# GLU output projection as seven products of 256 columns per index pair, placed behind a pass's quads, in a fused attention, rational and GLU kernel

## The chip, the cores and the metric

The kernel runs on one core of a Trainium2 chip. The metric is the device time of one execution in microseconds (us), median of the runs shown; lower is better. TensorE (PE, its weight loads shown as PEld), VectorE (DVE), ScalarE (ACT), GpSimd (POOL) and SyncE (SP, which issues all DMAs here) each run their own instructions in order and wait for each other by semaphores. SBUF is the on-chip memory, PSUM the banks into which TensorE writes.

## The reference, cut to what matters

```python
# attention with pooled keys and values, then x: 4608 tokens x 512
h = x @ w_in; P = a0 + a1*h + a2*h**2 + a3*h**3          # w_in: 512 x 2048
Q = 1 + abs(b0)*abs(h) + abs(b1)*h**2
x = (P / (Q + 1e-6)) @ w_out                              # the rational part
gate = 1 / (1 + np.exp(-(x @ w_gate)))                    # 512 x 1536
val  = x @ w_val                                          # 512 x 1536
out  = (gate * val) @ w_out2                              # 1536 x 512: the last projection
```

All of it is float32.

## The kernel before

**The rational part** covers attention and the first pair of projections. It runs 144 steps (`NB` = 9 blocks of 512 tokens by `NF1` = 16 slices of 128 hidden columns). A step is 12 matmuls of `g1` (hidden slice, bank h), a chain of ACT and DVE instructions to `y`, the split of `y` into a high part (ACT) and a low part `g` (POOL, L630), and 12 matmuls of `g2` (banks acc). Every product of float32 data is made as three TensorE passes, high by high, high by low and low by high. The order of this part is not written out: each instruction is handed to a planner (`Planner`) with an engine, a cost, a rank and its buffers, and the planner lays out the five engines' orders by these numbers. In the background of it, `background(u, ...)` for u = 0 to 11 reads a slice of the GLU's weights, converts it (`conv1`: two ACT, one DVE and one POOL instruction of 512 columns), makes the sums of weight blocks for seven products (`POOL`, L388), splits them (ACT L396, POOL L398) and stores them to DRAM (`w2d`). It also converts and splits slice u of `w_out2` (`conv2` with POOL, L309) and stores it (`wo2d`). The u-th is ranked at step 32 + 8u.

**The GLU part** is written out by hand. It has `NP` = 6 passes of 768 tokens, a pass in two halves of `HB` = 384 tokens. For each of `NS` = 6 index pairs `s_` (256 hidden columns as 2 slices of 128) a `gate` quad and a `value` quad are made. A quad forms a 2 by 2 block result, two hidden slices by two token halves, out of seven products (`ORDER`) with sums of weights and of inputs; it has 42 matmuls of 384 columns (6 per product). Its weights come through a ring of `NQ` = 6 tiles of 512 KB, 42 loads a pass. DVE adds the products up from PSUM (`quad_sums`, L897), ACT makes the sigmoid, and `value` multiplies and splits the result at once: two multiplications on DVE and two on POOL (L957), the high parts on ACT (L857), the low parts on POOL (L860). The split results are the stationary operand of the last projection: `h2(f, h, a)` does 3 token tiles by 3 matmuls of 512 columns for hidden slice f and token half h. The split `w_out2` lies in SBUF throughout (12 tiles). Half 0 is projected between the quads (`h2A(s_ - 1, p)`, behind `gate(s_, p)`), half 1 behind the last quad of the pass; between the two stands `x_prep`, which makes the seven input operands of the next pass (four sums on DVE, seven high parts on ACT, seven low parts on POOL, each of 768 columns). `h2_out` copies the finished 512-column banks out and stores them.

The quads take their banks from four "h" banks and at times b7; accA holds b4 to b6. A pass has 504 matmuls of 384 columns and 216 of 512.

## Time and profile before

| what | value |
|---|---|
| median of 3 runs (1762.6 to 1764.45) | 1762.63 us |
| profiled execution, its own time | 1762.16 us |
| its span, first to last instruction | 1760.4 us |
| granted TensorE clock, mean | 0.996 |
| matmuls in it | 9072 |

The span is 1.76 us short of the execution's own time. A page of the profile gives the busy time of each engine and the granted clock in 40 slices; a row of a timeline is a start, a duration, an engine, a line and what is written and read; a row of a window gives the busy time of each engine in a stretch. The duration of a matmul or a weight load in the trace is longer than its pace, since such instructions overlap: the pace is the distance between starts.

### The profile page before, as it was taken

What the parts mean: (1) busy time and instruction counts of PE and PEld (TensorE: products, weight loads), DVE (VectorE), ACT (ScalarE), POOL (GpSimd) and SP (SyncE); (2) the same over time, 40 slices, a digit from 0 to 9 for tenths busy, and PEclk for the clock granted to TensorE, in tenths of its full rate; (3) what the DMA queues carried; (4) which work ended last, traced back from release to release, by engine and by line L of the source; (5) the groups of instructions that cost most, each with busy time, mean ns of one, the idle gap of its engine ahead of it and who ended that gap; (6) DMA issues with size and microseconds to landing.
All of it is one profiled execution on the core that took longest, in us unless ns stands there. A gap on an engine that the chain in (4) does not pass through costs nothing.

```text
span 1760.4 us, 25436 instructions
## 1 busy us (share of the span) xinstructions
PE 1737.6 (99%) x9072; PEld 1524.8 (87%) x9072; DVE 1074.3 (61%) x1731; ACT 967.7 (55%) x1746; POOL 800.3 (45%) x827
## 2 busy tenths in 40 slices
PE   7899999999999999999999999999999999999999
PEld 6688888888888888888889999999998998998997
DVE  6998888888888878887874433443343333433341
ACT  5999778787888887877763222223223222222221
POOL 6675256464655745545522433344234324424331
PEclk8999999999999999999999999999999999999999
DMA  7685454556535554543755754764663763763660
GB/s 239 192 273 200 144 195 159 198 173 208 191 135 203 178 190 157 180 144 138 233 174 166 237 160 156 235 184 143 221 204 124 240 184 125 242 193 112 206 197 36
DMA packets 133329, 319.89 MB, mean 182 GB/s; under 512 B 20948, under 2 KB 51668, under 8 KB 133204
## 3 DMA queue, kind: packets, MB, share of 16 engines
q1 hardware_dynamic: 133204, 318.28, 55.6%
q8 instruction: 72, 1.18, 0.3%
q14 instruction: 53, 0.43, 0.1%
HBM read 263.20 MB, written 54.00 MB: 180 GB/s over the span
## 4 chain that ended last, share of the span: by engine, by line
PE 92%; ACT 3%; DVE 2%; DMA 2%; issue 0%; POOL 0%; SPq 0%; ACTq 0%; DVEq 0%
PE h L591 17%; PE h L593 17%; PE h L592 17%; PE acc L591 7%; PE acc L593 7%; PE acc L592 7%; PE accA L976 3%; PE accA L977 3%; PE h L977 3%; PE h L976 3%; PE accA L975 3%; PE h L975 3%; PE sc L540 2%; PE psx L576 2%; PE pta L565 1%
## 5 line engine op out<-in xcount | busy, mean ns | idle before, releaser
L897 DVE TENSOR_TENSOR t<-h,t 128x384 f32<-128x384 f32 x360 | 200.7, 557 | 376.7 <-ACT t L911 243.5
L630 POOL TENSOR_TENSOR g<-y,g 128x512 fp32r<-128x512 f32 x144 | 188.1, 1306 | 255.8 <-ACT g L629 196.8
L957 POOL TENSOR_TENSOR t<-t 128x384 f32<-128x384 f32 x72 | 84.2, 1170 | 439.7 <-issue 245.4
L591 PE MATMUL h<-xs,wi 128*128 128x512 f32 x576 | 229.6, 399 | 3.2 <-DVE wi L309 1.9
L591 PE MATMUL acc<-g,wo 128*128 128x512 f32 x576 | 230.6, 400 | 0.0
L593 PE MATMUL acc<-g,wo 128*128 128x512 f32 x576 | 224.9, 390 | 0.6 <-POOL g L630 0.6
L593 PE MATMUL h<-xs,wi 128*128 128x512 f32 x576 | 225.4, 391 | 0.0
L592 PE MATMUL h<-xs,wi 128*128 128x512 f32 x576 | 225.3, 391 | 0.0
L592 PE MATMUL acc<-g,wo 128*128 128x512 f32 x576 | 224.6, 390 | 0.0
L591 PE MATMUL h<-xS,wq 128*128 128x384 f32 x576 | 192.9, 335 | 0.6 <-DVE y L627 0.6
L593 PE MATMUL h<-xS,wq 128*128 128x384 f32 x576 | 192.9, 335 | 0.0
L592 PE MATMUL h<-xS,wq 128*128 128x384 f32 x576 | 192.7, 334 | 0.0
L911 ACT ACTIVATE t<-h 128x384 f32<-128x384 f32 x72 | 35.4, 492 | 243.2 <-PE h L593 240.6
L617 ACT ACTIVATE u<-h,coef 128x512 f32<-128x512 f32 x144 | 98.9, 687 | 88.5 <-PE h L593 87.9
L625 DVE SCALAR_TENSOR_TENSOR y<-y,coef,h 128x512 f32<-128x512 f32 x144 | 107.0, 743 | 62.1 <-ACT h L624 61.7
L591 PE MATMUL h<-xA,wq 128*128 128x384 f32 x432 | 144.4, 334 | 0.0
L593 PE MATMUL h<-xA,wq 128*128 128x384 f32 x432 | 144.3, 334 | 0.0
L592 PE MATMUL h<-xA,wq 128*128 128x384 f32 x432 | 144.3, 334 | 0.0
L619 DVE SCALAR_TENSOR_TENSOR u<-u,coef,h 128x512 f32<-128x512 f32 x144 | 106.8, 742 | 55.4 <-ACT y L618 54.2
L591 PEld LDWEIGHTS h<-xs,wi 128*128 128x128 f32 x576 | 108.9, 189 | 26.2 <-issue 2.6
L591 PEld LDWEIGHTS acc<-g,wo 128*128 128x128 f32 x576 | 108.2, 188 | 24.6 <-issue 3.4
L593 PEld LDWEIGHTS h<-xs,wi 128*128 128x128 f32 x576 | 108.8, 189 | 23.8
(119 smaller groups left out, 4090.9 us busy)
## 6 DMA issues: line engine op xcount, KB each, us to landing
wq<-w2d SPq DMA_DIRECT2D x252, 512.0 KB
wo<-wod SPq DMA_DIRECT2D x96, 512.0 KB
w2d<-stage SPq DMA_DIRECT2D x36, 512.0 KB
stage<-in_moe_w_out_dram SPq DMA_DIRECT2D x28, 512.0 KB
out_dram<-o SPq DMA_DIRECT2D x36, 256.0 KB
rawk<-in_k_dram SPq DMA_DIRECT2D x32, 256.0 KB
rawq<-in_q_dram SPq DMA_DIRECT2D x32, 256.0 KB
rawv<-in_v_dram SPq DMA_DIRECT2D x32, 256.0 KB
```

What stands on the lines that cost most here:

```text
L591: nc.tensor.matmul(out_, wl, xh, start=start, stop=False, skip_group_check=on)
L592: nc.tensor.matmul(out_, wh, xh, start=False, stop=False, skip_group_check=on)
L593: nc.tensor.matmul(out_, wh, xl, start=False, stop=stop, skip_group_check=on)
L617: ACT(0.57, rank, lambda: nc.scalar.activation(u.t, h.t, AF.Abs, scale=coef[:, 5:6]), w=[u], r=[h, coef_b])
L619: plan("DVE", 0.66, rank, lambda: STT(out=u.t, in0=u.t, scalar=coef[:, 4:5], in1=h.t, op0=ALU.add, op1=ALU.mult), w=[u], r=[h])
L625: plan("DVE", 0.66, rank, lambda: STT(out=y.t, in0=y.t, scalar=coef[:, 0:1], in1=h.t, op0=ALU.add, op1=ALU.mult), w=[y], r=[h])
L630: plan("POOL", 1.3, rank, lambda: nc.gpsimd.tensor_tensor(out=g.t[:, 1], in0=y.t, in1=g.t[:, 0].bitcast(F32), op=ALU.subtract), w=[(g, 1)] ...
L897: nc.vector.tensor_tensor(out=out_, in0=a, in1=b, op=ALU.add)
L957: eng.tensor_tensor(out=y, in0=x, in1=y, op=ALU.mult)
L975: nc.tensor.matmul(a[t], gh, wt[:, 0], start=(f == 0), stop=False)
L976: nc.tensor.matmul(a[t], gh, wt[:, 1], start=False, stop=False)
L977: nc.tensor.matmul(a[t], gl, wt[:, 0], start=False, stop=(f == NF2 - 1))
```

## The change

**The last projection** is made by the same seven-product scheme. The 2 by 2 blocks are two token halves by two hidden slices of a pair, times two hidden slices by two halves of 256 output columns; for each index pair that gives seven products of 3 token tiles by 3 matmuls of 256 columns. They run in `h2(p)` behind all twelve quads of a pass, kind by kind (`H2`): six index pairs of product 1, six of product 2, and so on, 42 units of 9 matmuls, 378 matmuls a pass. Two sets of three banks take turns (X and Y). At the end of a kind `cut` takes the banks out: ACT copies for kinds 1, 6 and 5, DVE additions and stores for kinds 2, 7 and 3, a copy and a store for kind 4, all of 256 columns.

**The operands** of it: `value` now writes the products of gate and value unsplit into twelve pairs of SBUF tiles (`ga`, `gx`), POOL adds one pair of blocks, and `first` makes the split of the operand of kind 1 (ACT high, POOL low) and a difference on POOL. The other 36 units are split in `h2` by `prep`, six units ahead: high part on ACT (L878), low part on DVE (L881); for kinds 5 and 7 DVE makes a difference first (L971), nine units ahead. Ahead of the unit loop `prep` is called for units 6 to 11, and the loop calls it for the same six again, so a pass has 42 such splits. Ahead of the loop the splits of units 9 to 11 wait for the matmuls of units 0 to 2, whose tiles they take.

**The weights** of it are no longer kept in SBUF. `item_load` reads 512 KB for two units at a time, six loads ahead, 21 a pass, on SP.

**x_prep** no longer has a place of its own: two sums go to POOL behind `value(3)` (`X_EARLY`), the other nine jobs stand between the units of `h2` (`X_AT`), with the low parts and the two sums on DVE.

**In the rational part** `background` no longer handles `w_out2`. `background_out(u, ...)`, ranked at step 100 + 3u, reads half of the rows' columns for a pair, converts it (`conv1`), makes four blocks of sums on POOL (L422: one instruction of 256 columns, two of 128), splits seven blocks of 128 columns (ACT and POOL, L427 and L429, in instructions of 512, 128 and 256) and stores seven pieces of 128 KB. The inputs of the first pass (`rawx`, the operands) are made eight steps later than before (`BX`).

```diff
+    def background_out(u, r0, gate_on):
...
+        conv1(raw, r0 + 2)
...
+            plan("POOL", pool(P * len(o)), r0 + 3, sub, w=[(t2, x) for x in o], r=rw + [(t2, x - 1) for x in o if x in (1, 3)])
...
+                plan("ACT", act(P * m), r0 + 3, lambda x=x, m=m, at=at, g=g: nc.scalar.activation(g.t[:, x:x + m, 0], at(), AF.Copy), w=[(g, (x, 0))], r=rt)
+                plan("POOL", pool(P * m), r0 + 3, lambda x=x, m=m, at=at, g=g: nc.gpsimd.tensor_tensor(
+                    out=g.t[:, x:x + m, 1], in0=at(), in1=g.t[:, x:x + m, 0].bitcast(F32), op=ALU.subtract), w=[(g, (x, 1))], r=rt + [(g, (x, 0))])
...
         def value(s_, p):
+            a12, a21, a11, a22 = (ga[m, s_] for m in ("12", "21", "11", "22"))
+
+            def first():
+                ops[s_] = o = op_tile(s_)
+                split_hi(o, a11)
+                split_lo(o, a11, nc.gpsimd)
+                sub(a11, a21, a11, nc.gpsimd)
...
+        H2 = ((1, "11", 0), (2, "12", 1), (6, "11", 0), (5, "21", 1), (7, "11", 0), (3, "12", 1), (4, "22", 0))
+        UNITS = [(k, m, s_) for k, m, _ in H2 for s_ in range(NS)]
...
+        def prep(x):
+            if x + 3 < len(UNITS):
+                k, m, s_ = UNITS[x + 3]
+                if k == 5:
+                    sub(ga["12", s_], ga["12", s_], ga["11", s_], nc.vector)
+                elif k == 7:
+                    sub(ga["11", s_], ga["22", s_], ga["11", s_], nc.vector)
+            if NS <= x < len(UNITS):
+                m, s_ = UNITS[x][1:]
+                ops[x] = o = op_tile(x)
+                split_hi(o, ga[m, s_])
+                split_lo(o, ga[m, s_], nc.vector)
+
+        def h2_mm(p, x, a, t):
...
+            nc.tensor.matmul(a, gh, wh, start=s_ == 0 and not on, stop=False, skip_group_check=on)
+            nc.tensor.matmul(a, gh, wl, start=False, stop=False, skip_group_check=on)
+            nc.tensor.matmul(a, gl, wh, start=False, stop=s_ == NS - 1, skip_group_check=on)
...
+            for x in range(NS, NS + AHEAD2):
+                prep(x)
...
+                for s_ in range(NS):
+                    x = g * NS + s_
+                    prep(x + AHEAD2)
+                    for t in range(HT):
+                        h2_mm(p, x, a, t)
+                    if x % 2:
+                        item_load(p * 7 * NS // 2 + x // 2 + NQ)
+                    if p + 1 < NP and x in X_AT:
+                        x_prep(X_LATE[X_AT.index(x)])
+                for t in range(HT):
+                    cut(t)
...
+        AHEAD2 = 6
...
             for s_ in range(1, NS):
                 gate(s_, p)
-                h2A(s_ - 1, p)
                 value(s_, p)
...
-            aB = [new_bank() for t in range(HT)]
-            for f in range(4):
-                h2(f, 1, aB)
-            if p + 1 < NP:
-                for x in range(4):
-                    x_prep(x)
-            h2A(NS - 1, p)
-            h2_out(p, 0, accA.pop(p))
-            for f in range(4, NF2):
-                h2(f, 1, aB)
-            h2_out(p, 1, aB)
+            h2(p)
```

How instructions stand now at three places. First TensorE at the end of a gate quad (xS is its last input operand, h its banks), before:

```order
L592 MATMUL h<-xS_8981,wq 128x384
L593 MATMUL h<-xS_8981,wq 128x384
L975 MATMUL accA<-wo_8978,gA 128x512
L976 MATMUL accA<-wo_8978,gA 128x512
L977 MATMUL accA<-wo_8978,gA 128x512
```

and with the change:

```order
L619 MATMUL h<-xS_9476,wq 128x384
L620 MATMUL h<-xS_9476,wq 128x384
L618 MATMUL h<-xS_9370,wq 128x384
L619 MATMUL h<-xS_9370,wq 128x384
L620 MATMUL h<-xS_9370,wq 128x384
```

The 18 matmuls of the projection that stood between the gate quad and the value quad are gone; the value quad follows at once.

Second VectorE from the last instructions of a pass's last value quad, in the first pass. Before (rawx are the input sums of `x_prep`, o the copies of `h2_out`, and then the next pass's quads):

```order
L957 TENSOR_TENSOR t<-t 128x384
L873 TENSOR_TENSOR rawx<-rawx 128x768 x4
L984 COPY o<-accA 128x512
L984 COPY o<-h 128x512
L897 TENSOR_TENSOR t<-h,t 128x384 x8
```

and with the change (go are the low parts for the projection, x the low parts of the next pass's inputs, L971 a difference):

```order
L989 TENSOR_TENSOR gx<-t 128x384
L881 TENSOR_TENSOR go<-ga,go 128x384 x2
L881 TENSOR_TENSOR go<-gx,go 128x384 x4
L881 TENSOR_TENSOR go<-ga,go 128x384 x2
L881 TENSOR_TENSOR go<-gx,go 128x384
L881 TENSOR_TENSOR xA_10533<-rawx,xA_10533 128x768
L881 TENSOR_TENSOR go<-gx,go 128x384 x3
L881 TENSOR_TENSOR go<-ga,go 128x384
L898 TENSOR_TENSOR rawx<-rawx 128x768
L881 TENSOR_TENSOR go<-ga,go 128x384 x2
L971 TENSOR_TENSOR ga<-ga 128x384
```

DVE had six instructions between the quads of two passes; now it starts on a row of splits, of which the seventh is the first that unit 6 needs, and goes on with the inputs of the next pass between them.

Third GpSimd in the rational part near step 114 of 144. Before (g is the low part of a step, e the attention, stage the weights):

```order
L630 TENSOR_TENSOR g<-y,g 128x512
L398 TENSOR_TENSOR stage<-stage 128x256
L309 TENSOR_TENSOR stage<-stage 128x512
L630 TENSOR_TENSOR g<-y,g 128x512
L557 TENSOR_TENSOR e<-e,r 128x8x72
```

and with the change:

```order
L657 TENSOR_TENSOR g<-y,g 128x512
L398 TENSOR_TENSOR stage<-stage 128x256
L422 TENSOR_TENSOR stage<-stage 128x2x128
L398 TENSOR_TENSOR stage<-stage 128x256
L422 TENSOR_TENSOR stage<-stage 128x128 x2
L429 TENSOR_TENSOR stage<-stage 128x4x128
L657 TENSOR_TENSOR g<-y,g 128x512
```

Between two low parts of steps stood two background instructions; now six stand there, the new sums (L422) and splits (L429) among them.

## Rows read from the trace of the kernel before

**Rows 1.** Page: span; TensorE's busy time; granted clock in 40 slices, in tenths.

```profile
span 1760.4 us, 25436 instructions
PE 1737.6 (99%) x9072; PEld 1524.8 (87%) x9072; DVE 1074.3 (61%) x1731; ACT 967.7 (55%) x1746; POOL 800.3 (45%) x827
PEclk8999999999999999999999999999999999999999
```

**Rows 2.** TensorE's waits from 900 us on: us in total, times, longest.

```profile
PE h L591 <- DVE y L627: 0.6, 1, 0.6
```

**Rows 3.** Windows: stretch, length, PE PEld DVE ACT POOL busy (instructions), clock, DMA share, GB/s.

```profile
943.39:1044.23 100.84, 100.84 (x553) 97.12 (x552) 39.49 (x66) 25.95 (x54) 32.94 (x32) 1.00 0.70 219
1044.23:1072.83 28.60, 28.60 (x127) 23.65 (x127) 9.57 (x8) 7.87 (x12) 18.15 (x12) 1.00 0.18 62
300.00:700.00 400.00, 399.85 (x2070) 329.55 (x2069) 332.05 (x549) 324.08 (x584) 227.73 (x272) 1.00 0.54 182
1520.00:1540.00 20.00, 20.00 (x111) 19.26 (x110) 8.03 (x14) 4.94 (x11) 7.57 (x8) 1.00 0.85 284
```

**Rows 4.** Timeline of TensorE: start us, duration us, line, tiles.

```profile
506.02 1.14 PE L540 MATMUL sc<-kbd,rawq 128*128 128x144 f32 x8
...
1018.22 0.33 PE L591 MATMUL h<-xS,wq 128*128 128x384 f32 x1
...
1032.81 0.39 PE L975 MATMUL accA<-wo,gA 128*128 128x512 f32 x1
...
1036.93 0.33 PE L591 MATMUL h<-xS,wq 128*128 128x384 f32 x1
...
1044.23 0.39 PE L975 MATMUL h<-wo,gB 128*128 128x512 f32 x1
...
1072.83 0.33 PE L591 MATMUL h<-xS,wq 128*128 128x384 f32 x1
```

**Rows 5.** One line's view, 500 to 508 us: duration min/median/max, first and last start.

```profile
L540 PE MATMUL sc<-kbd,rawq x8: 283/286/286, 506.0 to 506.9; 128*128 128x144 f32 x8
```

**Rows 6.** Groups of weight loads: line, tiles, shape, count, busy us, mean ns.

```profile
L540 PEld LDWEIGHTS sc<-kbd,rawq 128*128 128x128 f32 x320 | 46.1, 196 | 9.2 <-issue 3.2 <-ACT kbd L449 1.7 <-PE psx L576 1.3
L975 PEld LDWEIGHTS accA<-wo,gA 128*128 128x128 f32 x216 | 40.6, 188 | 7.8
```

**Rows 7.** Groups from 900 us on: line, tiles, shape, count, busy us, mean ns.

```profile
L897 DVE TENSOR_TENSOR t<-h,t 128x384 f32<-128x384 f32 x360 | 200.7, 557 | 376.7 <-ACT t L911 243.5 <-PE h L593 124.8
L857 ACT ACTIVATE gB<-t 128x384 fp32r<-128x384 f32 x42 | 22.1, 526 | 59.9 <-POOL t L957 59.9
L860 POOL TENSOR_TENSOR gB<-t,gB 128x384 fp32r<-128x384 f32 x42 | 42.7, 1017 | 26.7 <-PE h L593 15.3 <-ACT gB L857 11.5
```

**Rows 8.** Timeline of VectorE at five places, columns as in rows 4.

```profile
60.44 0.68 DVE L309 TENSOR_TENSOR wi<-stage,wi 128x512 fp32r<-128x512 f32 x1
61.04 0.45 DVE L546 TENSOR_TENSOR e<-sc,mx 128x288 f32<-128x288 f32 x1
...
1052.17 0.96 DVE L873 TENSOR_TENSOR rawx<-rawx 128x768 f32<-128x768 f32 x1 [2.71 <-POOL xA L860]
...
1087.62 0.56 DVE L897 TENSOR_TENSOR t<-h,t 128x384 f32<-128x384 f32 x1 [0.48 <-PE h L593]
1088.21 1.05 DVE L957 TENSOR_TENSOR t<-t 128x384 f32<-128x384 f32 x1
```

**Rows 9.** Groups of GpSimd and ScalarE from 500 to 900 us, columns as in rows 7.

```profile
L309 POOL TENSOR_TENSOR stage<-stage 128x512 fp32r<-128x512 f32 x7 | 9.2, 1315 | 0.7 <-ACT stage L307 0.6
L398 POOL TENSOR_TENSOR stage<-stage 128x256 fp32r<-128x256 f32 x48 | 35.3, 750 | 6.9 <-ACT stage L396 6.6
L388 POOL TENSOR_TENSOR stage<-stage 128x256 f32<-128x256 f32 x25 | 19.9, 817 | 0.6 <-DMA w2d<-stage 0.5
L396 ACT ACTIVATE stage<-stage 128x256 fp32r<-128x256 f32 x47 | 19.3, 420 | 1.1 <-POOL stage L388 1.1
```

**Rows 10.** Timeline at the end of the span: the last copy.

```profile
1756.63 0.60 ACT L982 ACTIVATE o<-h 128x512 f32<-128x512 f32 x1 [0.76 <-PE h L977]
```

More of the change, by code (lines that the diff above doesn't have):

```diff
@@ L809, in attention_moe_glu_kernel @@
             t.fn() if len(t.eng) == 1 else t.fn(t.on)
-        free_w = [s for s in slots["W"] if s not in [b.slot for b in list(ring.values()) + list(wo2.values())]]
+        free_w = [s for s in slots["W"] if s not in [b.slot for b in ring.values()]]
         free_w.sort(key=lambda s: plan.free[s])
-        assert len(ring) == NQ and len(wo2) == NF2 - 1
+        assert len(ring) == NQ and len(free_w) == NQ + 2 * NS + 1
         h_turn = sorted(slots["h"], key=lambda s: plan.free[s])
         ring_tag = {t: ring[t].slot for t in range(NQ)}
-        at_h, banks, tmps, turn = [-1], [0], [0], {"su": -1, "y": -1, "m": -1, "gA": -1}
+        cycle = h_turn + [f"b{x}" for x in range(4, 8)]
+        banks, tmps, turn = [-1], [0], {"su": -1, "y": -1, "m": -1}
         raw0 = rawx[0]
-        gs = {}
         def step(kind, n=3):
@@ L864, in x_load, with x_prep @@
                 nc.sync.dma_start(x_dst(h, d, m), x2d[ib].t[:, :, o:o + m])
-        def x_prep(part):
-            for job in X_PREP[part]:
-                if job[0] == "split":
-                    x = xo[job[1]] = late.tile([P, 2, 2, HB], F32R, tag="x" + job[1], name="x" + job[1])
-                    split_hi(x, half(*HALF[job[2]]))
-                    split_lo(x, half(*HALF[job[2]]), nc.gpsimd)
-                else:
-                    nc.vector.tensor_tensor(out=half(*HALF[job[1]]), in0=half(*HALF[job[2]]), in1=half(*HALF[job[3]]),
-                                            op=ALU.add if job[0] == "add" else ALU.subtract)
+        X_EARLY = X_PREP[0][1:3]
+        X_LATE = [job for part in X_PREP for job in part if job not in X_EARLY]
+        X_AT = (2, 6, 10, 24, 26, 28, 30, 32, 34)
+        def x_prep(job):
+            if job[0] == "split":
+                x = xo[job[1]] = late.tile([P, 2, 2, HB], F32R, tag="x" + job[1], name="x" + job[1])
+                split_hi(x, half(*HALF[job[2]]))
+                split_lo(x, half(*HALF[job[2]]), nc.vector)
+            else:
+                eng = nc.gpsimd if job in X_EARLY else nc.vector
+                eng.tensor_tensor(out=half(*HALF[job[1]]), in0=half(*HALF[job[2]]), in1=half(*HALF[job[3]]),
+                                  op=ALU.add if job[0] == "add" else ALU.subtract)
         def quad(u, p, cuts):
@@ new lines, in rows, with h2, cut @@
+        def rows(p, h, t, c):
+            r0 = (2 * p + h) * HB + t * P
+            return out[r0:r0 + P, 2 * P * c:2 * P * (c + 1)]
+        def h2(p):
+            Y, X = ([new_bank("acc") for t in range(HT)] for _ in range(2))
+            m1, um = {}, {}
+            for x in range(NS, NS + AHEAD2):
+                prep(x)
+            for g, (k, m, y) in enumerate(H2):
+                a = (X, Y)[y]
+                by_tile = g == 6 and p == NP - 1
+                def cut(t):
+                    c = a[t][:, :2 * P]
+                    if k == 1:
+                        m1[t] = new_tmp("m1")[:, :2 * P]
+                        nc.scalar.activation(m1[t], c, AF.Copy)
+                    elif k == 2:
+                        add(m1[t], c, m1[t])
+                        nc.sync.dma_start(rows(p, 0, t, 0), m1[t])
+                    elif k == 6:
+                        um[t] = new_tmp("um")
+                        nc.scalar.activation(um[t][:, :2 * P], c, AF.Copy)
+                    elif k == 5:
+                        nc.scalar.activation(um[t][:, 2 * P:], c, AF.Copy)
+                    elif k == 7:
+                        add(um[t][:, 2 * P:], c, um[t][:, 2 * P:])
+                        nc.sync.dma_start(rows(p, 1, t, 1), um[t][:, 2 * P:])
+                    elif k == 3:
+                        add(um[t][:, :2 * P], c, um[t][:, :2 * P])
+                        nc.sync.dma_start(rows(p, 0, t, 1), um[t][:, :2 * P])
+                    else:
+                        o = new_tmp("o")[:, :2 * P]
+                        if t % 2 and not by_tile:
+                            nc.vector.tensor_copy(o, c)
+                        else:
+                            nc.scalar.activation(o, c, AF.Copy)
+                        nc.sync.dma_start(rows(p, 1, t, 0), o)
+                if by_tile:
+                    for t in range(HT):
+                        for s_ in range(NS):
+                            h2_mm(p, g * NS + s_, a, t)
+                        cut(t)
+                    continue
+                for s_ in range(NS):
+                    x = g * NS + s_
[6 more added lines that the diff above has]
+                        x_prep(X_LATE[X_AT.index(x)])
+                for t in range(HT):
+                    cut(t)
+            for x in range(len(UNITS)):
+                ops.pop(x)
+                if x % 2:
+                    items.pop(p * 7 * NS // 2 + x // 2)
```

138 lines of the change are left out of this document (75 added, 63 removed).

## The prediction

> **What bounds the kernel now.** I read the page first: TensorE is busy for 1737.6 of 1760.4 us, at a granted clock of the full level (2.4 GHz) in all slices but the first [rows 1]. So whatever shortens the row of matmuls shortens the run, and whatever makes TensorE wait lengthens it. The waits come next: from 900 us on, which is the whole GLU part, the list of what TensorE waited for has one entry of 0.6 us [rows 2], and the windows of the first pass and of the rational part show TensorE busy throughout (100.84 of 100.84, 28.60 of 28.60, 399.85 of 400) [rows 3]. No other engine is near its limit in the GLU part: in the quads DVE has 39 us of work in 101, POOL 33 [rows 3]. So the sum is one of paces of matmuls, and every cost elsewhere counts only as far as it comes out as a new wait of TensorE.
>
> **The change part by part: the matmuls.** The pace is the distance between starts. From 1018.22 to 1032.81 there are 84 matmuls of 384 columns: 14.59/84 = 173.7 ns. From 1044.23 to 1072.83 there are 126 of 512: 227.0 ns; the 18 of a run between quads take 4.12 us, 228.9 ns each [rows 4]. At 2.4 GHz 384 columns are 160.0 ns and 512 are 213.3: both sizes carry the same 13.7 ns on top. So I put a matmul of 256 columns at 106.7 + 13.7 = 120.4 ns; this is the one estimate on which all rests, since the trace has no float32r matmul of that size. Before, a pass has 5 runs of 18 and one of 126: 90 x 228.9 + 126 x 227.0 ns = 49.2 us. With the change it has 378 x 120.4 ns = 45.5 us. Six passes: 295.2 - 273.1 = 22.1 us less. The 504 matmuls a pass of the quads stay. Bounds of the new pace: 119 ns from below (a little less on top than both sizes show), 122 from above, about the nearest pace of a short matmul with a full weight load: eight matmuls of the attention, of 144 columns, take 1.14 us [rows 4], the last of them 0.29 [rows 5], so they start 0.85/7 = 0.122 us apart. That gives 25.3 to 18.5 us.
>
> The Trainium skill ("TensorE: Matmul & The Clock Gate", Back-to-back issue gap) puts the gap of an isolated warm matmul at N/2.4 + 2.5 ns. By it 512 columns would take 215.8 ns, where the trace shows 227.0; if 256 columns kept to it (109.2 ns), the projection would take 2268 x 109.2 = 248 us, and the run would come out near 1717 us. The measured 13.7 ns decides for me.
>
> **The operands.** DVE takes over work in the projection. A pass has 42 low parts and 12 differences of 384 columns, nine instructions of 768 for the inputs, nine additions and one copy of 256. Two inputs from SBUF with POOL silent: 512 columns took 0.68 us, 768 took 0.96 [rows 8], so 384 are about 0.54 (straight line); beside a busy POOL 384 took 1.05 [rows 8]. An addition from PSUM of 384 is 557 ns [rows 7], so 256 are about 0.42. Sum: 54 x 0.54 + 9 x 0.96 + 10 x 0.42 = 42.0 us for 45.5 us of matmuls. It is covered, but just. Successive DVE instructions overlap by some 0.08 us (60.44 + 0.68 is past 61.04 [rows 8]), which helps. ACT has 42 x 0.526 [rows 7], seven of 768 (at most twice that), and eleven of 256 at 0.42 [rows 9], 34 us at most: covered.
>
> Two places are tight. **The first is unit 6.** Say the last value quad ends at T. At 1087.42 it did so in the trace, DVE added from +0.2 and multiplied from +0.8 to +1.8, slowed by POOL [rows 8]. POOL then still has a product, a sum, a low part and a difference of about 1.02 us each [rows 7], until about +4.3, so DVE's next splits are the slow kind: 2.9, 3.9, 4.7, then 5.2, 5.7, 6.2, and the one that unit 6 needs, seventh in the row, at 6.7. The splits of units 9 to 11 stand ahead of it and their ACT halves wait for units 0 to 2, the last until 3 x 1.08 + 0.5 = 3.8: no later than DVE. Unit 6 starts at 6 x 9 x 0.1204 = 6.5. So TensorE waits about 0.3 us a pass, 1.8 in all (0 to 1 a pass). Behind the waiting DVE stand the additions that free the banks and the stores on SP; the banks are wanted only one kind (6.5 us) later, and the six loads on SP that are ahead cover 13 us.
>
> **The second is units 12 to 26.** Between the split of unit 6 and that of unit 18 DVE has 12 splits, 4 differences, 3 instructions of 768 and 3 additions: 16 x 0.54 + 3 x 0.96 + 3 x 0.42 = 12.8 us, against 13.0 of matmuls; then a split and a difference per unit, 1.08 against 1.08. I take no wait here. If each instruction started 0.05 us later than that (no overlap, a semaphore between), some 1.8 us a pass would come out in the five passes with inputs: 9 us. That is the upper bound.
>
> **Quads without a projection between them.** A gate and a value quad last 14.6 us together; DVE has 12 instructions of about 0.56 in them and POOL five of about 1.02 to 1.3. The banks come back after eight turns, two quads, where before five served. Nothing late here: 0.
>
> **DMA.** A pass reads 42 tiles of 0.524 MB for quads and now 21 for the projection, 33 MB, with inputs and outputs 36 MB in 133 us: 272 GB/s. A stretch with 284 GB/s ran at 0.85 of the engines' time [rows 3], so there is room for about 330. In the quads it is one tile in 12 x 173.7 ns = 2.08 us (252 GB/s), in the projection one in 18 x 120.4 ns = 2.17 us; 219 GB/s ran at 0.70 with the first of these [rows 3]. With six loads ahead: 0. If it did come out, it would be by the whole difference of rates.
>
> **The rational part.** Per slice of `w_out2`, POOL had conversion and one split of 512 (1.315 us). Now it has sums of 0.817 and twice 128 columns, and splits of 1.315, 0.750 and 128 columns [rows 9]; 128 columns are about 0.47 (from 256 and 512): 4.29 us, 2.98 more, 36 us in all. It lies in 36 steps of 5.45 us (24 x 227 ns), where POOL had 57% of the time taken (227.73 of 400 [rows 3]): 3.1 us a step. With at most 1.3 us for the conversion, a slice took 2.6 us in eight steps and takes 5.6 in three: 3.1 - 0.3 + 1.9 = 4.7 us a step, 86%. Queued behind these on POOL is each step's low part, for which TensorE waits. The three steps between a low part's hidden slice and its use cover a burst. I take 1 us (0 to 10). The inputs that are made eight steps later cost nothing as long as POOL has four low parts left after them, as the order has it. The end: the last copy takes 0.60 us for 512 columns [rows 10] and about 0.42 for 256 [rows 9]: -0.2.
>
> **Sum**, against the profiled execution's own 1762.16 us (0.5 us under the median): -22.1 + 1.8 + 0 + 0 + 1.0 - 0.2 = -19.5, so 1742.7 us.
>
> **The rivals.** *A: DVE sets the pace of the projection.* The second place above goes wrong: 3 to 9 us of waits more. For it: 42 against 45.5 us with differences chained to splits; against: the overlap in rows 8 and POOL's silence there. 1746 to 1752, with a rational part at its bound 1757.
>
> *B, on the other side: GpSimd in the rational part.* If low parts of steps queue behind the added sums and splits, and these behind DMAs, TensorE waits for it between steps 100 and 136. All 36 us of added work on the path give 1743 + 36 = 1779, slower. It decides from 19 us on, when over half of the added work is uncovered. For it: 86% of an engine with in-order queues on both sides of it (DVE and ACT have 83% and 81% there [rows 3]). Against: the part is in the planner's hands with these costs in its tables, the three steps of slack, and TensorE's loss of 0.15 us in 400 before [rows 3].
>
> *C: the weight load sets the pace of a short matmul.* Each matmul reloads its 128 x 128 weights, and a load is recorded at 188 ns [rows 6]. With 512 columns it is hidden; if 256 columns cannot hide it, a matmul costs up to 188 ns: 2268 x 188 = 426 us for 295, and 1762 + 131 + 3 = 1896 us. It decides from 295.2/2268 = 130 ns on. Against: the attention's matmuls load as many columns, recorded at 196 ns [rows 6], and start 0.122 us apart [rows 4, 5]; at 384 columns the pace is 173.7, under the recorded load [rows 4]. The Trainium skill (same page, Measured speedup vs the span model) says weight loads overlap running matmuls only where row groups differ; here every load takes all rows. By that rule a load would stand between any two matmuls, and the trace disagrees: nothing of that size is between them at 512 or 384.
>
> *D: it does not save what it says.* The short matmul costs 125 to 130 ns, from a fixed cost that grows: within 4 us of before, 1759 to 1763.
>
> **How the numbers follow.** Forecast 0.68, A 0.17, B 0.06, C 0.05, D 0.04. The likeliest time is the forecast's, 1742.7, given as 1743. The low end is the pace of 119 ns without waits (1762.2 - 25.3 - 0.2 + 1 = 1738); the high end takes in A, 1757; B, C and D are left out, 0.15. A measurement of this kernel tells about 0.2% (3.5 us) from no change. Faster by more: forecast and A, 0.85. Within: D and a little of B, 0.05. Slower: most of B, and C, 0.10.
>
> **What would show it.** The matmuls of 256 columns should start 120 ns apart, and a projection should take 45.5 to 46.5 us from its first to its last. A wait of TensorE for DVE should stand at the first matmul of unit 6, 0 to 1 us, once a pass; more of them at units 12 to 26 speak for A. Waits of a step's matmuls for GpSimd between 560 and 800 us speak for B. Weight loads that end before each start, and a pace over 130 ns, speak for C. The granted clock should stay at 1.00. The prediction is wrong if the pace of the short matmuls is off by 3 ns or more (7 us), or if TensorE waits over 5 us anywhere.

## The result, and the profile of the changed kernel

The changed kernel takes 1742.55 us (median of 4 runs, 1742.33 to 1744.71); beside it the kernel before took 1762.64 us. The ratio is 0.9886, 95% interval 0.9869 to 0.9903: 20.1 us, or 1.1%, faster. The forecast was 1743.0 us in a range of 1738 to 1757. The profiled execution is the slowest of the four: its own time is 1744.71 us for a span of 1742.9. Its lines are read against the profiled execution before (1762.16 us).

From the page of the changed kernel, the lines that answer to [rows 1]: the span, the busy time of each engine, and the granted clock of TensorE in 40 slices.

```profile
span 1742.9 us, 28616 instructions
PE 1718.1 (99%) x10044; PEld 1555.2 (89%) x10044; DVE 1239.3 (71%) x2127; ACT 1047.6 (60%) x1957; POOL 750.7 (43%) x826
PEclk9899999999999999999999999999999999999999
```

TensorE is still the bound, now with 10044 matmuls instead of 9072 and 19.5 us less of busy time. DVE has 165 us more to do, GpSimd (POOL) 50 us less.

TensorE's waits from 930 us to the end, as in [rows 2] (us in total, times, longest):

```profile
PE acc L1031 <- DVE go L881: 1.8, 6, 0.3
PE h L618 <- DMA wq<-w2d: 1.7, 1, 1.7
PE acc L620 <- POOL g L657: 0.7, 1, 0.7
```

Where there was one wait there are now three kinds: six waits of 0.3 us for a low part from DVE, one per pass; one wait of 1.7 us for a tile of quad weights; and the last wait of the rational part, now for GpSimd's low part g (L657) where it was for DVE's y (L627).

Windows of the changed kernel, columns as in [rows 3]: the first pass's quads, its projection, the next pass's quads, the next projection.

```profile
945.20:1027.28 82.08, 80.36 (x464) 80.06 (x463) 36.95 (x66) 18.87 (x41) 31.41 (x29) 1.00 0.89 294
1027.28:1073.18 45.90, 45.60 (x379) 45.40 (x379) 40.05 (x75) 27.05 (x58) 4.66 (x4) 1.00 0.87 287
1073.18:1160.55 87.37, 87.37 (x507) 87.37 (x505) 39.30 (x71) 21.62 (x46) 31.42 (x29) 1.00 0.85 277
1160.55:1206.45 45.90, 45.60 (x379) 45.40 (x379) 40.05 (x75) 27.08 (x58) 4.66 (x4) 1.00 0.82 264
```

A projection takes 45.90 us from its first matmul to the next quad's first; before, 5 x 4.12 + 28.60 = 49.2 us [rows 4]. The 504 matmuls of a pass's quads take 87.37 us, 173.35 ns each. DVE is busy for 40.05 of the 45.90 us.

Timeline of TensorE in the first pass, columns as in [rows 4]: the late tile of quad weights, the projection's first matmul and its tenth, and three matmuls at unit 6, its second and third and the next.

```profile
981.43 0.41 PE L618 MATMUL h<-xA,wq 128*128 128x384 f32 x1 [1.72 <-DMA wq<-w2d]
...
1027.28 0.28 PE L1029 MATMUL acc<-wo,go 128*128 128x256 f32 x1
...
1028.34 0.28 PE L1029 MATMUL acc<-wo,go 128*128 128x256 f32 x1
...
1033.86 0.28 PE L1030 MATMUL acc<-wo,go 128*128 128x256 f32 x1
1034.44 0.39 PE L1031 MATMUL acc<-wo,go 128*128 128x256 f32 x1 [0.30 <-DVE go L881]
1034.66 0.28 PE L1029 MATMUL acc<-wo,go 128*128 128x256 f32 x1
```

The starts are 0.12 us apart, and at unit 6 there are 0.58 and 0.22 us where 0.12 and 0.12 would stand. It is the unit's third matmul that waits (L1031), the first that reads the low part. The wait is recorded as 0.30 us but costs 0.56 by the starts: the recorded idle time leaves out about a quarter of a microsecond. The late tile shows the same: it is recorded as 1.72 us, and the stretch lost 1.97 against a run without it (94.86 us for 92.89, below).

DVE from the end of the last value quad, in the same pass, GpSimd's last instruction beside it, and, after the gap, the end of DVE's work in the projection (start, duration, line):

```profile
1028.07 0.56 DVE L989 TENSOR_TENSOR gx<-t 128x384 f32<-128x384 f32 x1
1028.54 2.67 DVE L881 TENSOR_TENSOR go<-ga,go 128x384 fp32r<-128x384 f32 x2
1030.87 1.22 POOL L971 TENSOR_TENSOR gx<-gx 128x384 f32<-128x384 f32 x1
1031.13 1.38 DVE L881 TENSOR_TENSOR go<-gx,go 128x384 fp32r<-128x384 f32 x1
1032.43 1.48 DVE L881 TENSOR_TENSOR go<-gx,go 128x384 fp32r<-128x384 f32 x3
1033.84 1.01 DVE L881 TENSOR_TENSOR go<-ga,go 128x384 fp32r<-128x384 f32 x2
...
1066.87 1.08 DVE L922 TENSOR_TENSOR um<-acc,um 128x256 f32<-128x256 f32 x3
1073.02 0.42 DVE L1068 COPY o<-acc 128x256 f32<-128x256 f32 x1 [5.07 <-PE acc L1031]
```

This is the row of splits that the prediction walked through: three that start 1.30 us apart while GpSimd is busy (until 1032.09), then three 0.47 us apart, and the seventh, which unit 6 needs, begins at 1033.84 and ends near 1034.4. From 1067.95 on DVE idles for 5.07 us until the last copies.

**Where the 17.5 us between the two profiled executions went**, by starts of matmuls:

| stretch | before | after | difference |
|---|---|---|---|
| start to the 2401st of the 3456 matmuls of 512 columns in the rational part | 673.17 | 673.90 | +0.7 |
| from there to the last of them | 270.00 | 271.08 | +1.1 |
| from there to the first projection, without the 5 runs of 18 (20.60 us) before | 80.46 | 82.30 | +1.8 |
| six projections | 6 x 49.2 | 6 x 45.9 | -19.8 |
| quads of passes 1 to 5 | 5 x 87.52 | 5 x 87.37 | -0.7 |
| last matmul's start to the end of the span | 4.18 | 3.49 | -0.7 |

The sum is -17.6, against -17.5 between the spans. The first row's 0.7 us can't be put down to the change: the 769th of these matmuls, near the step where the part's weight work begins, started between 244.77 and 246.95 us in the eleven profiled executions of this kernel and of its variants that leave the rational part as it is, and 246.14 us before.

### The profile page after: what moved, and what is told of

Its sections match the earlier page's. It is cut to its first block, busy times and chain, and to the rows that moved or that the text cites. A ratio compares the mean times of both kernels' runs of the same rounds, so it can differ in the third digit from the quotient of the medians.

```text
span 1742.9 us, 28616 instructions
## 1 busy us (share of the span) xinstructions
PE 1718.1 (99%) x10044; PEld 1555.2 (89%) x10044; DVE 1239.3 (71%) x2127; ACT 1047.6 (60%) x1957; POOL 750.7 (43%) x826
## 4 chain that ended last, share of the span: by engine, by line
PE 90%; DVE 4%; DMA 3%; ACT 2%; issue 1%; POOL 0%; SPq 0%; DVEq 0%; ACTq 0%; POOLq 0%
PE h L618 17%; PE h L620 17%; PE h L619 17%; PE acc L618 7%; PE acc L620 7%; PE acc L619 7%; PE acc L1031 5%; PE acc L1029 4%; PE acc L1030 4%; PE sc L567 2%; DVE go L881 2%; PE psx L603 2%; PE pta L592 2%; DMA stage<-in_moe_w_gate_dram 1%; DMA wq<-w2d 1%
## 5 line engine op out<-in xcount | busy, mean ns | idle before, releaser
L657 POOL TENSOR_TENSOR g<-y,g 128x512 fp32r<-128x512 f32 x144 | 187.5, 1302 | 201.3 <-ACT g L656 157.9
L989 POOL TENSOR_TENSOR ga<-t 128x384 f32<-128x384 f32 x48 | 48.8, 1017 | 434.6 <-DVE t L922 434.6
L1031 PE MATMUL acc<-wo,go 128*128 128x256 f32 x756 | 214.8, 284 | 1.8 <-DVE go L881 1.8
L1029 PE MATMUL acc<-wo,go 128*128 128x256 f32 x756 | 214.2, 283 | 0.0
L1030 PE MATMUL acc<-wo,go 128*128 128x256 f32 x756 | 214.1, 283 | 0.0
L1031 PEld LDWEIGHTS acc<-wo,go 128*128 128x128 f32 x756 | 145.2, 192 | 3.0 <-DVE go L881 3.0
L618 PE MATMUL h<-xA,wq 128*128 128x384 f32 x432 | 144.6, 335 | 1.7 <-DMA wq<-w2d 1.7
L1030 PEld LDWEIGHTS acc<-wo,go 128*128 128x128 f32 x756 | 145.2, 192 | 0.0
L1029 PEld LDWEIGHTS acc<-wo,go 128*128 128x128 f32 x756 | 145.2, 192 | 0.0
```

Of the source, the lines that this page charges most:

```text
L618: nc.tensor.matmul(out_, wl, xh, start=start, stop=False, skip_group_check=on)
L657: plan("POOL", 1.3, rank, lambda: nc.gpsimd.tensor_tensor(out=g.t[:, 1], in0=y.t, in1=g.t[:, 0].bitcast(F32), op=ALU.subtract), w=[(g, 1)] ...
L989: eng.tensor_tensor(out=dst, in0=x, in1=y, op=ALU.mult)
L1029: nc.tensor.matmul(a, gh, wh, start=s_ == 0 and not on, stop=False, skip_group_check=on)
L1030: nc.tensor.matmul(a, gh, wl, start=False, stop=False, skip_group_check=on)
L1031: nc.tensor.matmul(a, gl, wh, start=False, stop=s_ == NS - 1, skip_group_check=on)
```

## The experiments

**The cost of 128 columns, and what a weight load is worth.** The forecast rests on a pace of 120 ns, and the rival with the largest price said that the weight load sets the pace from some size on. So each matmul of 256 columns was made as two of 128:

```diff
-            a = a[t][:, :2 * P]
-            nc.tensor.matmul(a, gh, wh, start=s_ == 0 and not on, ...)
+            for c in range(2):
+                b = a[t][:, c * P:(c + 1) * P]
+                vh, vl = (y[:, c * P:(c + 1) * P] for y in (wh, wl))
+                nc.tensor.matmul(b, gh, vh, start=s_ == 0 and not on, ...)
...
```

> Every matmul of 256 columns of the last projection is made as two of 128 columns: 756 a pass for 378, the same products and the complete result. If the time on top of the columns stays at 13.7 ns, a matmul takes 53.3 + 13.7 = 67 ns, a pass's projection 50.7 us for 45.6, and the run 1742.5 + 6 x 5.1 = 1773 us. If the weight load (145 ns as recorded now, 188 before) sets the pace from some size on, at least 107 ns, the pace of 256 columns without what is on top: 81 us a pass and 1742.5 + 212 = 1955 us or more; at 145 ns 110 us a pass and 2127 us. Between 67 and 107 ns the load would be hidden in part.

It took 1973.84 us, 231 us more than the changed kernel, and a pass's projection 84.37 us: 111.6 ns a matmul. The 145 ns of the expectation is a misreading: 145.2 is the busy time in us of a group of 756 loads in the changed kernel's profile, and the recorded mean of one load is 192 ns. So its second figure, 2127 us, falls away; the first, 1955 us or more, held. Both halves of a bank opened their sums with the start flag, and the result was incomplete, unlike what the expectation says; the next run has the flag in the first half alone.

```diff
-                nc.tensor.matmul(b, gh, vh, start=s_ == 0 and not on, ...)
+                nc.tensor.matmul(b, gh, vh, start=s_ == 0 and not on and c == 0, ...)
```

> As the kernel with two matmuls of 128 columns for each of 256, but only the first half of a bank opens its sum with the start flag; in the run before, both halves opened theirs, and the second took the first half's first products out of the sum, so its output was incomplete. Theory: the flag has no part in the time; 84.4 us a pass, 111.6 ns a matmul, some 1974 us, and the result is complete. Rival: opening sums in two halves of a bank cost the time; then less, down to 1773 us.

It took 1975.63 us (one run, as the next two kernels), and a projection again 84.37 us. A window of 20 us in its first projection, columns as above:

```profile
1040.00:1060.00 20.00, 20.00 (x182) 20.00 (x181) 13.60 (x27) 6.15 (x12) 0.00 (x0) 1.00 0.55 152
```

No engine is near its limit but TensorE, at the full clock: the 111.6 ns are its own. 128 columns at 2.4 GHz are 53.3 ns, so the 13.3 to 13.7 ns on top that were measured at 256, 384 and 512 columns do not hold here.

**192 and 64 columns.** Is 111.6 ns a floor, or a flatter slope below 256 columns? Two kernels leave columns out of each product and keep the weight loads (and drop the splits that are made twice):

```diff
+            n = 192   # and 64 in the other kernel
+            f = s_ == 0 and not on
+            m = 2 * P if f else n
+            nc.tensor.matmul(a[:, :m], gh, wh[:, :m], start=f, ...)
+            nc.tensor.matmul(a[:, :n], gh, wl[:, :n], start=False, ...)
+            nc.tensor.matmul(a[:, :n], gl, wh[:, :n], start=False, ...)
```

> The last projection's matmuls do 192 of their 256 columns (all but the first one of each bank; the last 64 columns of each product are left out, so the output is not the reference's), and the six splits that are made twice are deleted. The weight load of each matmul stays. Theory (a floor set by the weight load, 111.6 ns as 128 columns showed): 369 x 111.6 + 9 x 120 ns = 42.3 us a pass for 45.35, 1740.9 - 6 x 3.1 = 1722 us. Rival 1 (columns at 2.4 GHz + 13.3 ns all the way down to a much lower size, 93.3 ns): 35.5 us of matmuls, held up by DVE's 37.3 us, 38 to 40 us, 1697 to 1709 us. Rival 2 (a straight line from 111.6 at 128 to 120.0 at 256 columns): 115.8 ns, 43.8 us, 1732 us.

192 columns: 1720.85 us, a projection of 42.24 us, for the 42.3 that the floor gives; the straight line would have given 43.8. So 192 columns cost the same 111.6 ns as 128.

> As the one with 192 columns, but with 64 of 256 (the other columns of each product are left out, so the output is not the reference's). Floor theory: the pace is again 111.6 ns, 42.3 us a pass, 1722 us, the same as with 192 columns. If the floor is only a slower slope below 256 columns (8.4 ns per 128 columns): 107.4 ns, 40.7 us a pass, 1713 us. If columns still counted in full below 128: 85 ns, and DVE sets the pace at 38 to 40 us, 1697 to 1709 us.

64 columns: 1940.07 us, which none of the three expectations had. Windows of that kernel: the first 5.47 us of the first projection, 40 us within it, and 70 us of the next pass's quads.

```profile
1026.53:1032.00 5.47, 5.47 (x51) 5.47 (x50) 5.24 (x6) 2.71 (x6) 4.59 (x4) 1.00 0.91 324
1040.00:1080.00 40.00, 40.00 (x189) 40.00 (x189) 19.70 (x38) 15.43 (x31) 0.00 (x0) 0.50 0.48 144
1110.00:1180.00 70.00, 70.00 (x405) 70.00 (x404) 32.35 (x58) 15.93 (x33) 29.26 (x26) 1.00 0.84 274
```

TensorE never waits in this projection, yet some 6.5 us into it the granted clock falls from 1.00 to 0.50, the lower of its two levels, 1.2 GHz. The starts are 111.6 ns apart before that and 213.3 ns after. So the floor theory held as long as the clock did, and at half the clock the floor is about twice as high. The six projections took 74.6 to 77.6 us each. With 128 and 192 columns the clock stayed at 1.00 in the projections.

What follows: at the full clock the pace of these matmuls is the larger of two, columns at 2.4 GHz plus some 13.3 ns, and a floor of 111.6 ns. The floor does not depend on the columns (64, 128 and 192), while each matmul keeps its load of 128 x 128 weights. That the width of the load sets it is the author's reading; it is not shown, since no run here changes the load. The Trainium skill ("TensorE: Matmul & The Clock Gate", LDWEIGHTS (loading the stationary operand)) gives P/1.2 ns for a load of P columns, 106.7 ns for 128; the measured 111.6 ns lie 4.9 ns above that, and the 213.3 ns at the lower clock are twice that. The recorded duration of a load, 192 ns in the changed kernel and 188 in [rows 6], is no such price. By an estimate from these two, the paces cross at (111.6 - 13.3) x 2.4 = 236 columns, so the 256 of the change lie just on the side where the columns set the pace.

One place in the trace of the kernel before speaks against the width of the load. The attention's transposes load 72 columns, not 128, with 128 columns streamed:

```profile
195.57 1.03 PE L565 MATMUL pta<-ident,e 128*72 128x128 f32 x8
L565 PEld LDWEIGHTS pta<-ident,e x40: 112/114/116, 195.3 to 255.1; 128*72 128x72 f32 x40
```

The last of the eight lasts 0.27 us, so they start (1.03 - 0.27)/7 = 0.109 us apart: nearly the floor, with a load of little over half the width, recorded at 114 ns. They are transposes of plain float32 data, so they do not decide it either. A floor that goes with each pair of a load and a matmul, whatever the load's width, is a rival that no run here excludes.

**The splits that are made twice.** The seventh split is late at unit 6. Is it late because six splits stand ahead of it that the loop makes again, or because GpSimd is beside DVE?

```diff
-            for x in range(NS, NS + AHEAD2):
-                prep(x)
```

> The six splits ahead of the projection's unit loop, which the loop makes again, are deleted; the result is complete. My theory: DVE then makes unit 6's split as its first instead of its seventh after the pass's last value quad, so the wait of TensorE at unit 6 (0.3 us a pass, 1.8 in all) is gone; each of them costs about 0.35 us in starts, so -2 us: 1740.5 against 1742.5. Rival: DVE is late there because GpSimd is beside it, not because of six more instructions; the wait stays, 1742.5.

1740.9 us (ratio 0.9876 to before, 0.9862 to 0.9891). The projections of this kernel (the first and the second), and TensorE's waits from 900 us on:

```profile
1024.99:1070.33 45.34, 45.34 (x379) 45.34 (x379) 37.30 (x69) 24.59 (x52) 4.65 (x4) 1.00 0.90 289
1159.09:1204.44 45.35, 45.35 (x379) 45.35 (x379) 37.30 (x69) 24.60 (x52) 4.66 (x4) 1.00 0.86 267
```

```profile
PE h L618 <- DMA wq<-w2d: 1.8, 3, 1.1
PE acc L620 <- POOL g L657: 0.7, 1, 0.7
```

No wait for DVE is left and a projection takes 45.35 us for 45.90: 0.55 us a pass, 3.3 in all. So without the six splits that are made twice the wait is gone, although GpSimd is as busy as before. That does not clear GpSimd: beside it three splits of the row start 1.30 us apart instead of 0.47, 2.5 us in all, and by this estimate the seventh would have been in time with GpSimd silent too. So by that estimate the wait needed both; no run has GpSimd silent. This run also gives the pace of a pure row: 45.35/378 = 120.0 ns. Of the 3.3 us it gives back a part: three waits for weight tiles lie in the quads of the passes (1.8 us by the record, 2.6 by the starts), where the changed kernel had one.

**The late tile of quad weights.** The trace's 1.7 us at 981 us were in no term of the sum.

```diff
-                if p == 0:
-                    item_load(s_ - 1)
-                    if s_ == NS - 1:
-                        item_load(s_)
+                if p == 0 and s_ >= 3:
+                    item_load(2 * s_ - 6)
+                    item_load(2 * s_ - 5)
```

> In the first pass alone the six loads of the last projection's weights come two each in the index pairs 3, 4 and 5, not one each from pair 1 on. Theory: the wait of 1.7 us of TensorE for a tile of quad weights at 981 us comes of the 0.5 MB that each such load adds while the next pass's inputs are loaded too; it goes, -1.7 us: 1740.8, and no wait stands later, since the tiles are wanted only after the last quad. Rival: the ring of quad weights starts the GLU part too empty and the wait stays or moves, 1742.5 or up to 2 us more.

1741.93 us (0.9884, 0.9868 to 0.9901). TensorE's waits from 900 us on:

```profile
PE acc L1031 <- DVE go L881: 1.7, 6, 0.3
PE acc L620 <- POOL g L657: 0.7, 1, 0.7
PE h L618 <- DMA wq<-w2d: 0.5, 2, 0.3
```

The wait in the first pass is gone: from its first quad to its projection it takes 92.89 us for 94.86. Two short waits stand in the fourth and the fifth pass instead, 0.5 us of starts each. The median lies between the theory's 1740.8 and the rival's 1742.5; it is 0.6 us under that of the changed kernel, which is within the spread of the runs.

**Both edits.**

> The first two edits together: no splits made twice, and the first pass's loads of projection weights in pairs 3 to 5. If both theories hold, TensorE has no wait over 0.7 us left from 930 us on, and the time is 1742.5 - 2.0 - 1.7 = 1738.8 us. If the one or the other rival holds, 1740.5 to 1741; if both do, 1742.5.

1738.33 us (0.9865, 0.985 to 0.988), close to the 1738.8 of both theories together. Of TensorE's waits from 900 us on one is left:

```profile
PE acc L620 <- POOL g L657: 0.7, 1, 0.7
```

**The changed kernel and both edits side by side,** since a quarter of a per cent is at stake.

> The changed kernel as it is, on the same chip and beside the same runs of the kernel before as the version with both edits, since the two differ by a quarter of a per cent. If the stage lengths of the first trace hold (45.9 us a projection, 1.8 to 2 us lost for a tile of quad weights in the first pass or less): 1741.5 to 1743.5 us. Rival (its one profile drew an unusual wait): the DMA wait of the first pass is under 1 us, 1740.5 to 1741.5.

1742.19 us (0.9892, 0.9877 to 0.9907). In its profile there is no late tile at all:

```profile
PE acc L1031 <- DVE go L881: 1.8, 6, 0.3
PE acc L620 <- POOL g L657: 0.7, 1, 0.7
```

So of the wait the rival was right, though the time is in the theory's range: the wait of 1.7 us comes in some executions and not in others. The stretch from the first quad to the first projection was 92.97 us here; in the other kernels with the loads from pair 1 on and the same order in the rational part, it was 93.38, 93.54, 93.73, 93.99, 94.01 and 94.92; with the loads in pairs 3 to 5 it was 92.89, 92.89 and 93.03. Of the eight executions with the loads from pair 1 on, the profiled one of the change (94.86) and this one among them, seven lost 0.5 to 2.0 us; in six of these a wait for a tile is recorded, in one a wait for DVE. None of the three with later loads lost more than 0.14.

> The version with both edits again, beside the changed kernel. Theory: projections of 45.35 us and first-pass quads of 92.9 us, so it is below the changed kernel by 6 x 0.54 + 0.9 to 2 = 4.1 to 5.2 us by the trace, 1737.5 to 1739. Rival: without the wait at unit 6 the quads of later passes wait for weight tiles instead, as they did for 1.8 us with the first edit alone, and the gain is 2 to 3 us.

1740.37 us (0.9875, 0.9859 to 0.9892). The expected 1737.5 to 1739 was too low, and its rival is not the reason: all six projections take 45.35 us and the quads of passes 1 to 5 87.37, and the GLU part has no wait. From the second pass's first quad to the last matmul it needs 663.45 us, the changed kernel beside it 666.22: 2.77 us, five times 0.55. What this execution lost is in the rational part, which both kernels have alike: from the 769th to the 2401st matmul it took 428.26 us for 426.85 beside it, and from there to the last 273.03 for 271.02. By the trace both edits are worth 3.3 us, and up to 2 more where a tile would have been late; the median is 1.8 us under that of the changed kernel beside it, and that of the first run of this version 4.2 us under the changed kernel's first. Against the kernel before beside it, this version is 22.95 and 21.4 us faster in its two runs, the changed kernel 20.1 and 19.6 in its two. It is the fastest version with a complete result, by a margin near the spread of the runs.

**The place of the weight sums in the rational part.** Was the dense placement, 3 steps a pair from step 100, a cost of GpSimd?

```diff
-    OR, OS, BX = 4 * SEG + 68, 3, 8
+    OR, OS, BX = 4 * SEG, 8, 8
```

> The weight sums of the last projection are ranked one pair per 8 steps from step 32 on, as the last projection's plain splits were before the change, not one per 3 steps from step 100. My theory: the dense placement costs TensorE nothing in the rational part, so the spread-out one gives the same within 1 us: 1741.5 to 1743.5. Rival (GpSimd is crowded at 86% between steps 100 and 136 and delays TensorE): several us faster, 1733 to 1739. Third possibility: the sums now meet the quads' weight work of the same steps on GpSimd and on the DMA queues, several us slower.

1740.12 us (0.988, 0.9865 to 0.9894), 2.4 us under the changed kernel's first median and 2.1 under its second: between the theory and its rival. Windows from the 2401st to the last matmul of 512 columns of the rational part, of this kernel and then of the changed one (PE PEld DVE ACT POOL as above):

```profile
672.15:941.08 268.93, 268.93 (x1338) 223.38 (x1337) 213.46 (x335) 208.26 (x364) 133.23 (x140) 1.00 0.45 147
```

```profile
673.90:944.98 271.08, 269.67 (x1339) 223.31 (x1338) 215.50 (x342) 223.32 (x404) 173.63 (x196) 1.00 0.60 190
```

Spread out, TensorE does not wait once in this stretch; dense, it waits twice, 1.4 us in all:

```profile
859.11 0.50 PE L618 MATMUL acc<-g,wo 128*128 128x512 f32 x1 [0.73 <-ACT o L681]
930.01 0.50 PE L620 MATMUL acc<-g,wo 128*128 128x512 f32 x1 [0.68 <-POOL g L657]
```

One of the two is for ScalarE, which has 223.3 us of work for 208.3, the other for GpSimd, which has 173.6 for 133.2. So the dense placement does cost TensorE something there, but only half of it is GpSimd's. Both waits stand in all eleven profiled executions with the dense placement. The spread-out one has one profiled execution. In it the stretch before, from the 769th matmul to the 2401st, takes 429.03 us with the sums spread out, for 427.41 without them: over both stretches 697.97 us for 698.50. The rest of the lower time comes from the time before (the 769th matmul at 243.12 us for 246.48), and most of that is there at the first of these matmuls already (30.21 us for 32.40). By these two executions the placement moves a cost of 1 to 2 us and does not remove it.

**DVE's headroom in the projection.** Each split in the loop makes its low part twice (and the six ahead of the loop are deleted):

```diff
                 split_lo(o, ga[m, s_], nc.vector)
+                split_lo(o, ga[m, s_], nc.vector)
```

> The six splits ahead of the loop are deleted, and each of the 36 splits in the loop makes its low part twice on DVE (the second overwrites the first with the same values): 36 x about 0.5 = 18 us more of DVE a pass, 6 x 0.5 = 3 less. It measures how near DVE is to setting the pace. DVE had 40.1 us of work in the 45.6 us of the projection and was done 5.2 us before its end. With 40.1 + 18 - 3 = 55 us of work, TensorE should wait 8 to 11 us a pass: 1742.5 + 6 x 9.5 = 1800 us (1790 to 1809). If DVE already set the pace (rival A): all of 15 us, 1833 us. If much of DVE's time is slack by overlap: under 1780.

1814.48 us (ratio 1.0295, 1.0278 to 1.0312). A projection takes 58.30 us instead of 45.35. A window over the second, and TensorE's wait for DVE in all:

```profile
1172.06:1230.35 58.29, 50.70 (x379) 47.40 (x379) 56.82 (x105) 24.19 (x52) 4.65 (x4) 0.97 0.60 193
```

```profile
PE acc L1032 <- DVE go L881: 44.4, 100, 1.2
```

DVE is now the bound: 56.82 us of work in 58.29. (The clock of 0.97 in this window is no part of it: the first projection took 58.30 us at 1.00.) The time is above the expected range of 1790 to 1809. DVE got 19.5 us more work than in the kernel without the double splits, 36 x 0.54 (0.5 was expected, which is 9 of the 14 us above 1800), and the projection 12.95 us; the 6.6 us between are slack that DVE had. By this estimate there was room for some 12 more instructions of this kind a pass (6.6/0.54). The changed kernel itself, with 40.05 us of work for 37.30, had 3.8 us left.

## Why the prediction was right

The time came out 0.45 us from the forecast, and the mechanism is the one that was forecast: fewer columns in all, at 120 ns for a matmul of 256, and a short wait for DVE at unit 6. That it came out so near is luck. In the profiled execution, the slowest of the four, the terms add up to -17.6 us for the -19.5 of the sum, with single terms off by 1 to 2 us in both directions, and the median execution is 2.2 us below that one.

**Matmuls, -22.1 predicted.** Measured with no wait in the row: 6 x (45.35 - 49.2) = -23.1. 120.4 ns was put, 120.0 came, inside the bounds of 119 and 122. That the time on top of the columns carries over was right at this size and would have been wrong below some 236 columns; the prediction did not see how near that is. The rule of the Trainium skill for an isolated matmul that the prediction set aside (same page, Back-to-back issue gap, N/2.4 + 2.5 ns) gives 109.2 ns here; the trace disagrees, with 120.0.

**Unit 6, +1.8 predicted.** The wait is there, for the seventh split, 0.3 us by the record, six times. That the recorded length agrees is in part chance: the split was ready some 7.1 us after the projection's start and not at 6.7, since the three slow splits took 1.30 us each, and it was needed at the unit's third matmul and not at its first, 0.24 us later. The price was mis-sized: 0.55 us a pass, 3.3 in all, as the kernel without the wait shows. The idle time in front of a matmul is about 0.25 us less than what the row of starts loses.

**Units 12 to 26, 0 (up to 9).** No wait there. Rival A needed DVE to fall behind. DVE had 40.05 us of work (42.0 was put) and was done 5.07 us before its last copy, and the run with 36 more instructions shows where A would have begun: some 3.8 us of work more than the changed kernel has.

**Quads, 0.** They came out 0.15 us a pass faster, 173.35 ns a matmul for 173.7 with the projection's runs between them.

**DMA, 0.** This step failed in the profiled execution: a tile was 1.7 us late in the first pass, 1.97 by the starts. The prediction compared rates of a whole pass, and a rate says nothing of one late tile. In that window the queues moved 294 GB/s at 0.89 of the engines' time, above the 284 at 0.85 that the estimate took as well below the limit [rows 3]. The loads of projection weights are the part of it that the change added, and with them later the wait in the first pass was gone in three of three executions. Waits for a tile of 0.25 to 1.13 us by the record stand in later passes too, in three of the variants. Why it comes in one execution of the same kernel and not in the next stays open.

**The rational part, +1 (0 to 10).** Measured +1.1; in the eleven profiled executions with the dense placement the stretch took 270.6 to 273.0 us for 270.0, a middle of +1.3. Rival B (from 19 us of uncovered work on) is out: TensorE's one recorded wait for GpSimd there is 0.7 us. The prediction looked for B's waits between 560 and 800 us; steps 100 to 136 lie at 674 to 893, and in all of 560 to 893 the profiled execution has one wait, that for ScalarE at 859. GpSimd was busy for 150.5 of the 221.5 us from 673.9 on, 0.68 and not 0.86: a step there takes 6.1 us, more than its 24 matmuls of 512 columns.

**The tail, -0.2 predicted.** Measured -0.7. The last copy is shorter by the 0.2 us (0.38 us for 0.60); From the last matmul's start to the end of that copy it takes 0.70 us for 1.02, and from there to the end of the span, where the last store stands, 2.80 for 3.15.

**Rival C** was priced wrongly, though it did not decide. It took the recorded 188 ns as what a load can cost; the floor is 111.6 ns. So it would have cost nothing here, and at 128 columns, where columns and the time on top would give 67 ns, 45 ns a matmul. The prediction's reason against C, the attention's pace of 0.122 us at 144 columns [rows 4, 5], does not speak against it: 144 columns and the time on top are 73 ns, so it is not the columns that set that pace either. That it came out at 122 ns and not 111.6 was not followed up. The sentence on overlap that the prediction takes from the Trainium skill there stands in that page's section The mechanism.

**Rival D** (125 to 130 ns) is out with 120.0.

## What to carry to other kernels

Before a matmul is cut into smaller ones, compare the pace at two sizes that the trace has; what is on top of the columns carries over, but only down to the floor of matmuls that each have their own weight load, here 111.6 ns or some 236 columns. Do not price that floor by the recorded duration of a load. Add to each recorded wait of TensorE what the starts around it lose beyond it, here about 0.25 us (0.30 recorded cost 0.56, 1.72 cost 1.97), and look ahead of it for work that is done twice. A DMA term that is "room in the mean rate" should carry a range: at 0.85 to 0.9 of the engines' time single tiles were late in some executions, at a cost of 0.5 to 2 us.

## What the runs showed of the hardware that was not expected

A row of matmuls that never waits can still lose the clock: with 64 columns for each load of 128 x 128 weights the granted clock fell to 0.50 some 6.5 us into the projection, and the starts went from 111.6 to 213.3 ns; it was back at 1.00 in the quads between 1110 and 1180 us. With 128 and 192 columns and the same loads it stayed at 1.00.

With a start flag on the second half of a bank, while the sum in the first half was open, the result was incomplete. Opening the bank once, with the first half's first matmul, gave the whole result, at the same 84.37 us a projection. That the second flag took out what the first half had summed so far is the reading that fits; the runs do not show which products went.

The start of an execution is a source of spread by itself: the first matmul of 512 columns started between 31.1 and 33.7 us in the eleven profiled executions that share one rational part, 2.6 us apart, which is near what either edit is worth. The lengths of the projections, and of quads in which no tile was late, repeat to a few hundredths of a microsecond; they told the edits apart where the medians did not.
